# Sliding-window attention and a highway layer: key chunks shifted by half a block, scores packed by 64x64 quadrants

## The chip, the cores and the metric

The kernel runs on one core of one Trainium2 chip. The metric is the device time of one execution in microseconds. A profiled execution also gives a trace of each engine: TensorE (PE, with its weight loads as PEld), VectorE (DVE), ScalarE (ACT), GpSimd (POOL, which here mostly issues loads) and SyncE (SP, which issues stores).

## The reference

Two layers follow each other: attention in which each query sees the first four keys ("sinks") and the 128 latest, then a highway layer on the rows of all heads joined.

```python
# q, k, v: (B=4, H=8, S=768, D=64); n_sink = 4, window = 128
scores = (1 / sqrt(D)) * (q @ k.transpose(0, 1, 3, 2))
keep = (pos_k < n_sink) | ((pos_q - pos_k >= 0) & (pos_q - pos_k < window))
a = softmax(where(keep, scores, -1e9))
x = (a @ v).transpose(0, 2, 1, 3).reshape(B * S, H * D)      # 3072 x 512
h = maximum(x @ w_h, 0)
t = 1 / (1 + exp(-(x @ w_t + b_t)))
out = t * h + (1 - t) * x
```

## The kernel before

The 3072 rows are cut into 24 chunks of 128 (six per batch entry); chunk n is `n % 6` within its batch entry. A chunk goes through these steps, which the code names by engine:

- `load_qk`, `load_v` (lines 81, 90): POOL issues three DMAs that bring 128 rows of q, k and v for all heads and turn f32 into f16. `AHEAD = 8` chunks are loaded ahead.
- `pe_T` (193): eight transposes make q and k columns of 128 rows, two heads to a 128x128 block, in one PSUM tile from the pool `m_ps`; `act_T` (202) copies all 1024 columns to SBUF on ACT as `qk`.
- `pe_S` (233): scores, keys on partitions and queries on columns. The keys a query block can see lie in the chunk before and in its own chunk, so there are 256 score columns for each head, half of which the window masks. A chunk takes 16 matmuls, 8 for each half-chunk of four heads (half as many in the first chunk of a batch entry). Each head has 64 rows of contraction, so even heads use rows 0 to 63 of the array and odd heads rows 64 to 127, into different PSUM banks.
- `act_S` (248): exp of 1024 columns per half-chunk, twice a chunk. `dve_mask` (257): multiply by a 0/1 mask. The first chunk of a batch entry has only its own keys, 512 columns.
- `pe_sink`, `act_sink` (216, 226): scores of the four sinks of all heads for two chunks at once, needed for chunks 2 to 5 of a batch entry (`ks`, which `pool_sink` fills, line 207; sink values `vs` by `sink_v`).
- `pe_A` (267): 16 matmuls of 66 columns, e times v and a column that sums the weights; two more for the sinks. `dve_rec`, `dve_x` (292, 297): divide, giving `xh`.
- `pe_X`, `act_X` (309, 316): four transposes of `xh`, copied to SBUF by ACT as `xT`.
- `pe_Mh`, `pe_Mt` (337, 321): the two products with the weights, four matmuls of 512 columns each (and one for the bias). `act_u` (332): tanh. `dve_d`, `dve_e`, `dve_o` (345, 351, 357): the highway combination; SP stores 128 rows.

PSUM holds two score tiles of two banks (`ps_s`), one A tile of two banks (`ps_av`), and two banks (`ps_m`) that turn among transposes, sink scores, Mh and Mt. The order of the work on each engine is that of the program text: lines 379 to 486 write it out by hand, and each engine takes its instructions in that order. In the loop, iteration i does T(i+2), S(i+1), X(i-1), A(i), Mh(i-1), Mt(i-1) on PE; ACT takes qk(i+2), xT(i-1), the two exps of i+1, u(i-1); DVE takes the masks of i+1, ee, otok, rec, xh, dd. Iterations -2 to 1 are written apart for the start, where the first stage also multiplies zeros (`warm_up(8)`, `spare(3)`).

The POOL queue at the start (137 to 162) is: q0, k0, the identity's mask, v0, q1, k1, two selects that make the 0/1 mask, v1, the sink values, the weights w_t and w_h, two small selects, and then the further chunks. `more_constants` (166 to 178) is DVE work that waits for the mask.

Of the kernel before, what the change touches and what calls it, by code (L numbers as in the profile page):

```python
# [8 lines left out]
FP16 = mybir.dt.float16  # L9
# [7 lines left out]
_AVN = 66  # L17
# [3 lines left out]
def kernel(  # L21
# [40 lines left out]
    sd_pool = ctx.enter_context(tc.tile_pool(name="p_sd", bufs=AHEAD))  # L62
    qkT_pool = ctx.enter_context(tc.tile_pool(name="p_qkT", bufs=5))
    e_pool = ctx.enter_context(tc.tile_pool(name="p_e", bufs=5))
    r_pool = ctx.enter_context(tc.tile_pool(name="p_r", bufs=3))
    x_pool = ctx.enter_context(tc.tile_pool(name="p_x", bufs=7))
# [6 lines left out]
    NV = AHEAD + 4  # L73
    NS4 = H * NSINK
    KW = NHP * P + 32
    XBAR = ()
    LATE = 0
    v_ring = [const.tile([P, VW], FP16, tag=f"v{i}", name=f"v{i}") for i in range(NV)]
    qk_sd = {}

    def load_qk(n):
        b, c = divmod(n, NSC)
        rows = slice(c * P, (c + 1) * P)
        qsd = sd_pool.tile([P, H, D], FP16, tag="qsd", name="qsd")
        ksd = sd_pool.tile([P, H, D], FP16, tag="ksd", name="ksd")
        nc.gpsimd.dma_start(out=qsd, in_=q[b, :, rows, :].transpose([1, 0, 2]))  # L86
        nc.gpsimd.dma_start(out=ksd, in_=k[b, :, rows, :].transpose([1, 0, 2]))  # L87
        qk_sd[n] = (qsd, ksd)

    def load_v(n):  # L90
        b, c = divmod(n, NSC)
        rows = slice(c * P, (c + 1) * P)
        vt = v_ring[n % NV][:, 0:H * 65].rearrange("p (h e) -> p h e", e=65)
        nc.gpsimd.dma_start(out=vt[:, :, 0:D], in_=v[b, :, rows, :].transpose([1, 0, 2]))  # L94
# [8 lines left out]
    mask = const.tile([P, 2, P], FP16, tag="mask", name="mask")  # L103
    mask0 = const.tile([P, P], FP16, tag="mask0", name="mask0")
    mask1 = const.tile([P, 2, P], FP16, tag="mask1", name="mask1")
# [5 lines left out]
    ones_row = const.tile([P, P], FP16, tag="ones_row")  # L111
    ks_bd = [const.tile([P, KW], FP16, tag=f"ks{i}", name=f"ks{i}") for i in range(2)]
    vs_bd = [const.tile([P, H, 65], FP16, tag=f"vs{i}", name=f"vs{i}") for i in range(2)]
    vs_dn = [const.tile([NS4, D], FP16, tag=f"vd{i}", name=f"vd{i}") for i in range(2)]
    es_t = [const.tile([P, 2, P], FP16, tag=f"es{i}", name=f"es{i}") for i in range(2)]

    with tc.manual_schedule(engines={ENG.DVE}):
        nc.vector.memset(warm, 0.0)
        nc.vector.memset(ident, 1.0)
        nc.vector.memset(ebias, _EXP_BIAS)  # L120
        nc.vector.memset(mask, 1.0)
        nc.vector.memset(bm, 1.0)
        for vt in v_ring:
            init_v(vt)

    def load_sink_v(b):
        nc.gpsimd.dma_start(out=vs_dn[b % 2], in_=v[b, :, 0:NSINK, :])

    def sink_v(b, eng):
        eng.tensor_tensor(  # L130
            out=vs_bd[b % 2][0:NS4, :, 0:D], in0=vs_dn[b % 2].unsqueeze(1).to_broadcast([NS4, H, D]),
            in1=bm[0:NS4, :].unsqueeze(2).to_broadcast([NS4, H, D]), op=ALU.mult)
# [4 lines left out]
    with tc.manual_schedule(engines={ENG.Pool}):  # L137
        load_qk(0)
# [4 lines left out]
        load_qk(1)  # L143
        nc.gpsimd.affine_select(
            out=mask[:, 1, :], in_=mask[:, 1, :], compare_op=ALU.is_ge, fill=0.0,
            base=0, pattern=[[1, P]], channel_multiplier=-1)
        nc.gpsimd.affine_select(
            out=mask[:, 0, :], in_=mask[:, 0, :], compare_op=ALU.is_ge, fill=0.0,
            base=-1, pattern=[[-1, P]], channel_multiplier=1)
        load_v(1)  # L150
        load_sink_v(0)
        load_w(moe_w_t, wt_sb)
# [7 lines left out]
        load_qk(2)  # L160
        load_v(2)
        load_qk(3)

    nc.sync.dma_start(out=bt32, in_=moe_b_t.unsqueeze(0))

    def more_constants():
# [7 lines left out]
        nc.vector.tensor_copy(out=mask0, in_=mask[:, 1, :])  # L174
        nc.vector.memset(mask0[0:NSINK, :], 1.0)
        nc.vector.tensor_copy(out=mask1, in_=mask)
        nc.vector.memset(mask1[0:NSINK, 0, :], 1.0)
# [12 lines left out]
    qkT, tp_of, s_of, e_of, av_of, rec_of = {}, {}, {}, {}, {}, {}  # L190
    xtp_of, xh_of, xT_of, t_of, u_of, h_of, dd_of, ee_of, sk_of = {}, {}, {}, {}, {}, {}, {}, {}, {}

    def pe_T(n):
        qsd, ksd = qk_sd.pop(n)
        tp = m_ps.tile([P, 2 * NHP, P], FP16, tag="m", name="tp")
        for j in range(NHP):
            nc.tensor.transpose(tp[:, j, :], qsd[:, 2 * j:2 * j + 2, :], ident)  # L197
        for j in range(NHP):
            nc.tensor.transpose(tp[:, NHP + j, :], ksd[:, 2 * j:2 * j + 2, :], ident)  # L199
        tp_of[n] = tp  # L200

    def act_T(n):
        qk = qkT_pool.tile([P, 2 * NHP, P], FP16, tag="qk", name="qk")
        nc.scalar.copy(out=qk, in_=tp_of.pop(n))  # L204
        qkT[n] = (qk[:, 0:NHP, :], qk[:, NHP:2 * NHP, :])

    def pool_sink(b):
        _, kT = qkT[b * NSC]
        ks = ks_bd[b % 2]
        for hh in range(2):  # L210
            rows = slice(64 * hh, 64 * hh + 64)
            dst = ks[rows, 0:NHP * 136].rearrange("p (a b) -> p a b", b=136)
            nc.gpsimd.tensor_copy(out=dst[:, :, NSINK * hh:NSINK * hh + NSINK],
                                  in_=kT[rows, :, 0:NSINK])

    def pe_sink(n):
        ks = ks_bd[(n // NSC) % 2]
        sk = m_ps.tile([P, 2, P], FP32, tag="m", name="sk")
        for t in range(2):
            qT, _ = qkT[n + t]  # L220
            for hp in range(NHP):
                nc.tensor.matmul(sk[:, t, :], lhsT=ks[:, hp * P:(hp + 1) * P],
                                 rhs=qT[:, hp, :], start=(hp == 0), stop=(hp == NHP - 1))
        sk_of[n] = sk

    def act_sink(n):
        nc.scalar.activation(out=es_t[(n // 2) % 2][0:NS4], in_=sk_of.pop(n)[0:NS4], func=AF.Exp,
                             bias=ebias[0:NS4], scale=SCALE)

    def srcs_of(n):  # L230
        return ([] if n % NSC == 0 else [qkT[n - 1][1]]) + [qkT[n][1]]

    def pe_S(n, g):
        qT, _ = qkT[n]
        srcs = srcs_of(n)
        np_ = len(srcs)
        sps = s_ps.tile([P, 2, 512], FP32, tag="s", name="sps")
        for hl in range(2):
            hp = 2 * g + hl
            for pc, kk in enumerate(srcs):  # L240
                for hh in range(2):
                    rows = slice(64 * hh, 64 * hh + 64)
                    o = (hl * np_ + pc) * P
                    nc.tensor.matmul(sps[:, hh, o:o + P], lhsT=kk[rows, hp, :],  # L244
                                     rhs=qT[rows, hp, :], start=True, stop=True)
        s_of[n, g] = sps

    def act_S(n, g):
        np_ = 1 if n % NSC == 0 else 2
        sps = s_of.pop((n, g))  # L250
        e = e_pool.tile([P, 2, 2, np_, P], FP16, tag="e", name="e")
        nc.scalar.activation(out=e.rearrange("p a b c d -> p a (b c d)"),  # L252
                             in_=sps[:, :, 0:2 * np_ * P], func=AF.Exp,
# [3 lines left out]
    def dve_mask(n, g):  # L257
        c = n % NSC
        np_ = 1 if c == 0 else 2
        m = {0: mask0, 1: mask1.rearrange("p a b -> p (a b)")}.get(  # L260
            c, mask.rearrange("p a b -> p (a b)"))
        ev = e_of[n, g].rearrange("p a b c d -> p (a b) (c d)")
        nc.vector.tensor_tensor(  # L263
            out=ev, in0=ev, in1=m.unsqueeze(1).to_broadcast([P, 4, np_ * P]),
            op=ALU.mult)

    def pe_A(n, warm_n=0):
        b, c = divmod(n, NSC)
        vts = ([] if c == 0 else [v_ring[(n - 1) % NV]]) + [v_ring[n % NV]]
        av = av_ps.tile([P, 2, 4, P], FP32, tag="av", name="av")  # L270
        for _ in range(warm_n):
            nc.tensor.matmul(av[:, 0, :, :], lhsT=warm[:, 0:P], rhs=warm, start=True, stop=True)
        for g in range(2):
            e = e_of.pop((n, g))
            first = True
            for hl in range(2):
                for hh in range(2):
# [244 lines left out]
```

The softmax here doesn't subtract the row's maximum and nothing guards it: scores larger than these inputs give would overflow.

## Time and profile before

| | us |
|---|---|
| median of three runs | 130.05 (129.35 to 130.19) |
| the profiled execution, its own time | 129.52 |
| span of its trace, first to last instruction | 127.8 |
| first scores, S(0) | 7.97 |
| first A matmul of chunk 4 | 34.43 |
| first A matmul of chunk 23 | 115.78 |
| last output operation ends, on DVE | 124.4 |

The page of the profile gives each engine's busy time and its share of the span, the chain that ended last, and the costliest groups: line, engine, operation, tile written and read, count, then busy time, the mean duration of one in ns, and the idle time before them with what ended it. In the order of time, a row has the start and the length of a run of equal instructions. Matmuls overlap: a matmul's length is its passage through the array, and the next one starts long before it ends, so what a block costs is the distance to the start of the next block.

### The profile page before, as it was taken

To read this page: it belongs to the slowest core of one execution; us is meant where nothing else is said; L and a number is where in the kernel's file an instruction comes from. 1 tells how busy PE (TensorE), PEld (TensorE's weight loads), DVE (VectorE), ACT (ScalarE), POOL (GpSimd) and SP (SyncE) were. 2 spreads that over 40 slices of the span, in tenths; PEclk is the share of its full clock that TensorE was granted. 3 is DMA by queue.
4 is the path that set the end of the run, shared out by engine and by line. 5 is a ranking of instruction groups with operands and counts; after the bars stand their busy time and mean duration, and the time that the engine had idled before them with its cause. 6 is when DMAs were issued, how large, how long until landed. Compare 5 with 4: busy or idle time off the path is not lost.

```text
span 127.8 us, 3253 instructions
## 1 busy us (share of the span) xinstructions
PE 110.1 (86%) x1315; PEld 67.9 (53%) x1315; DVE 101.8 (80%) x214; ACT 97.6 (76%) x129; POOL 74.9 (59%) x98
## 2 busy tenths in 40 slices
PE   6758989569999899999998999999989999999620
PEld 2236434447755574586555656755655666564300
DVE  6544626495999898998998998989989999899760
ACT  4066435999897998998987989989969989893310
POOL 6999939999899989999999995005000000000000
PEclk9999999999999999999999999999999999999996
DMA  0999999999999999999999999922022202210222
GB/s 1 105 126 140 165 153 157 180 181 197 160 156 204 204 180 201 163 199 200 164 199 194 208 159 205 186 95 82 8 82 82 82 5 82 82 60 28 82 82 82
DMA packets 79728, 17.00 MB, mean 133 GB/s; under 512 B 75617, under 2 KB 76641, under 8 KB 79714
## 3 DMA queue, kind: packets, MB, share of 16 engines
q0 software_dynamic: 76256, 10.51, 122.6%
q1 hardware_dynamic: 3458, 6.30, 13.3%
q8 instruction: 10, 0.16, 0.5%
q14 instruction: 4, 0.03, 0.1%
HBM read 21.01 MB, written 6.29 MB: 214 GB/s over the span
## 4 chain that ended last, share of the span: by engine, by line
PE 39%; ACT 29%; DMA 12%; POOL 9%; DVE 6%; issue 3%; POOLq 0%; ACTq 0%
PE tps L328 14%; PE hps L341 11%; ACT qk L204 10%; DMA wh_sb<-in_moe_w_h_dram 7%; ACT u L334 6%; ACT e L252 6%; ACT xT L318 5%; DMA ksd<-in_k_dram 5%; PE tps L326 4%; POOL qsd L86 3%; PE sps L244 3%; PE av L280 2%; POOL ksd L87 2%; POOL v L94 2%; PE xtp L313 2%
## 5 line engine op out<-in xcount | busy, mean ns | idle before, releaser
L252 ACT ACTIVATE e<-sps,ebias 128x1024 f16<-128x1024 f32 (+1 forms) x48 | 48.6, 1054 | 1.8 <-PE sps L244 1.8
L263 DVE TENSOR_TENSOR e<-e,mask 128x1024 f16<-128x1024 f16 (+1 forms) x48 | 29.1, 640 | 4.7 <-ACT e L252 4.6
L204 ACT COPY qk<-tp 128x1024 f16<-128x1024 f16 x24 | 24.2, 1009 | 6.4 <-PE tp L199 6.4
L341 PE MATMUL hps<-wh_sb,xT 128*128 128x512 f16 x96 | 24.8, 380 | 3.4 <-ACT xT L318 2.9
L334 ACT ACTIVATE u<-tps 128x512 f16<-128x512 f32 x24 | 14.3, 597 | 16.0 <-PE tps L328 16.0
L328 PE MATMUL tps<-wt_sb,xT 128*128 128x512 f16 x96 | 25.0, 384 | 0.1
L86 POOL DMA_DIRECT2D qsd<-in_q_dram x24 | 22.4, 932 | 3.4 <-DMA wh_sb<-in_moe_w_h_dram 2.0
L94 POOL DMA_DIRECT2D v<-in_v_dram x24 | 22.3, 929 | 0.5 <-DVE dd L347 0.3
L347 DVE SCALAR_TENSOR_TENSOR dd<-hps,xh 128x512 f16<-128x512 f32 x24 | 16.6, 691 | 7.4 <-PE hps L341 5.7
L87 POOL DMA_DIRECT2D ksd<-in_k_dram x24 | 22.1, 920 | 0.5 <-PE tps L328 0.3
L353 DVE SCALAR_TENSOR_TENSOR ee<-u,dd 128x512 f16<-128x512 f16 x24 | 16.5, 689 | 3.5 <-ACT u L334 3.2
L280 PE MATMUL av<-v,e 128*128 128x66 f16 x352 | 17.7, 197 | 0.6 <-DVE e L263 0.5
L328 PEld LDWEIGHTS <-xT 128*128 128x128 f16 x96 | 9.4, 98 | 15.0 <-issue 4.1
L299 DVE TENSOR_TENSOR xh<-av,rec 128x512 f16<-128x512 f32 x24 | 16.6, 692 | 0.8
L359 DVE SCALAR_TENSOR_TENSOR otok<-xh,ee 128x512 f32<-128x512 f16 x24 | 16.6, 692 | 0.8
L280 PEld LDWEIGHTS <-e 128*128 128x128 f16 x352 | 15.2, 100 | 2.2 <-DVE e L263 1.9
L244 PE MATMUL sps<-qk 64*128 64x128 f16 x352 | 14.6, 223 | 1.5 <-ACT qk L204 1.5
L318 ACT COPY xT<-xtp 128x512 f16<-128x512 f16 x24 | 14.4, 598 | 0.4 <-PE xtp L313 0.3
L341 PEld LDWEIGHTS <-xT 128*128 128x128 f16 x96 | 7.9, 97 | 12.0 <-ACT xT L318 5.7
L244 PEld LDWEIGHTS <-qk 64*128 64x128 f16 x352 | 10.4, 97 | 4.8 <-ACT qk L204 1.4
L199 PE MATMUL tp<-ident,ksd 128*128 128x128 f16 x96 | 9.8, 227 | 1.7 <-DMA ksd<-in_k_dram 1.6
L197 PEld LDWEIGHTS <-qsd 128*128 128x128 f16 x96 | 7.2, 100 | 6.8 <-DMA qsd<-in_q_dram 2.2
(51 smaller groups left out, 100.2 us busy)
## 6 DMA issues: line engine op xcount, KB each, us to landing
out_dram<-otok SPq DMA_DIRECT2D x24, 256.0 KB, 4.5
qsd<-in_q_dram POOLq DMA_DIRECT2D x24, 128.0 KB, 6.5
ksd<-in_k_dram POOLq DMA_DIRECT2D x24, 128.0 KB, 6.5
v<-in_v_dram POOLq DMA_DIRECT2D x24, 128.0 KB, 6.7
wt_sb<-in_moe_w_t_dram POOLq DMA_DIRECT2D x1, 512.0 KB, 7.3
wh_sb<-in_moe_w_h_dram POOLq DMA_DIRECT2D x1, 512.0 KB, 9.4
vd<-in_v_dram POOLq DMA_DIRECT2D x4, 4.0 KB, 4.9
bt<-in_moe_b_t_dram SPq DMA_DIRECT2D x1, 2.0 KB
```

The source lines that it names most:

```text
L86: nc.gpsimd.dma_start(out=qsd, in_=q[b, :, rows, :].transpose([1, 0, 2]))
L87: nc.gpsimd.dma_start(out=ksd, in_=k[b, :, rows, :].transpose([1, 0, 2]))
L94: nc.gpsimd.dma_start(out=vt[:, :, 0:D], in_=v[b, :, rows, :].transpose([1, 0, 2]))
L204: nc.scalar.copy(out=qk, in_=tp_of.pop(n))
L244: nc.tensor.matmul(sps[:, hh, o:o + P], lhsT=kk[rows, hp, :], rhs=qT[rows, hp, :], start=True, stop=True)
L252: nc.scalar.activation(out=e.rearrange("p a b c d -> p a (b c d)"), in_=sps[:, :, 0:2 * np_ * P], func=AF.Exp, bias=ebias, scale=SCALE)
L263: nc.vector.tensor_tensor(out=ev, in0=ev, in1=m.unsqueeze(1).to_broadcast([P, 4, np_ * P]), op=ALU.mult)
L280: nc.tensor.matmul(av[:, g, 2 * hl + hh, 0:_AVN], lhsT=e[:, hh, hl, pc, :], rhs=vt[:, 65 * h:65 * h + _AVN], start=first, stop=False, skip ...
L318: nc.scalar.copy(out=xT, in_=xtp_of.pop(n))
L328: nc.tensor.matmul(tps, lhsT=xT[:, kc, :], rhs=wt_sb[:, kc, :], start=False, stop=(kc == NOC - 1))
L334: nc.scalar.activation(out=u, in_=t_of.pop(n), func=AF.Tanh)
L341: nc.tensor.matmul(hps, lhsT=xT[:, kc, :], rhs=wh_sb[:, kc, :], start=(kc == 0), stop=(kc == NOC - 1))
```

## The change

Keys and values are cut at other places than queries. Query chunk c still covers rows 128c to 128c + 127, but key chunk c covers rows 128c - 64 to 128c + 63 (`chunk_parts`). At the seam of two batch entries a key chunk has 64 rows of each, loaded by two DMAs; there are 25 key chunks instead of 24. The 128 queries of a block then see all of their own key chunk in part ("A"), the upper half of the queries sees the lower half of the next key chunk, and the lower half of the queries the upper half of the chunk before ("B"). The two B parts are 64x64 squares and share 64 columns, one on partitions 0 to 63 and one on 64 to 127, so a head has 192 score columns (`EW`) instead of 256.

The parts that change with it:

- exp, mask and `e` have 768 columns per half-chunk, in all chunks (the first chunk of a batch entry too, with its own mask).
- `pe_SA` takes 8 matmuls of 128 columns a chunk, `pe_SB` 16 of 64 columns on 64 rows and 64 columns of the array. `pe_AA` takes 8 and `pe_AB` 16 matmuls of 66 columns, the latter on 64x64 quadrants in pairs.
- `pe_T` transposes q or k in 64-row halves, 8 transposes of 64 columns for each, into the last 512 bytes of the two banks of a score tile, where 768 of 1024 columns are used. `act_T` copies 512 columns; q on ACT, k on ACT in the loop and mostly on DVE at the start.
- In the loop, T of chunk n+2 is hosted by the score tiles of chunk n; `xT` is copied by DVE; X(i) stands at the end of iteration i, and dd, ee, otok run for i-2.
- Sink scores are needed for chunk 1 too: two chunks at once in later batch entries, one at a time in the first. The four sink-value loads go to SP at the start.
- The start is written anew (`lone_T`, `lone_S`), w_h is loaded ahead of w_t, the three spare matmuls go, the pool sizes change (q/k landing 10, transposed q and k 7 each, x 5).

```diff
+    def chunk_parts(n):
+        b, c = divmod(n, NSC)
+        if c:
+            return [(slice(0, P), b, c * P - HP)]
+        return ([(slice(0, HP), b - 1, S - HP)] if b else []) + ([(slice(HP, P), b, 0)] if b < B else [])
...
-        load_qk(0)
+        nc.sync.dma_start(out=bt32, in_=moe_b_t.unsqueeze(0))
+        for b in range(B):
+            nc.sync.dma_start(out=vs_dn[b], in_=v[b, :, 0:NSINK, :])
+        load_q(0)
+        load_k(0)
+        load_k(1)
         nc.gpsimd.affine_select(
             out=ident, in_=ident, compare_op=ALU.is_equal, fill=0.0,
             base=0, pattern=[[-1, P]], channel_multiplier=1)
         load_v(0)
...
+        load_v(1)
+        load_q(1)
+        load_k(2)
+        tri(mask, slice(0, HP), 0, P, HP - 1, -1, 1)
+        tri(mask, slice(HP, P), 0, P, 0, 1, -1)
+        tri(mask, slice(0, HP), P, EW, 0, 1, -1)
+        tri(mask, slice(HP, P), P, EW, -1, -1, 1)
         load_w(moe_w_h, wh_sb)
...
+    def t_view(sps):
+        return sps.bitcast(FP16)[:, :, 4 * EW:4 * EW + 4 * HP].rearrange(
+            "p h (a b) -> p h a b", b=HP)
+
+    def pe_T(n, g, sd):
...
+        tv = t_view(s_tile(n, g))
+        for hp in range(NHP):
+            for hf in range(2):
+                rows = slice(HP * hf, HP * hf + HP)
+                nc.tensor.transpose(tv[:, hf, hp, :], sd[rows, 2 * hp:2 * hp + 2, :],
+                                    ident[rows, rows])
...
+    def pe_SA(n, g):
+        sps = s_tile(n, g)
         for hl in range(2):
             hp = 2 * g + hl
-            for pc, kk in enumerate(srcs):
+            for hh in range(2):
+                rows = slice(64 * hh, 64 * hh + 64)
+                nc.tensor.matmul(sps[:, hh, hl * EW:hl * EW + P], lhsT=kT[n][rows, hp, :],
+                                 rhs=qT[n][rows, hp, :], start=True, stop=True)
+
+    def pe_SB(n, g):
+        sps = s_tile(n, g)
+        prev = kT[n - 1] if n % NSC else kT[n]
+        for hl in range(2):
+            hp = 2 * g + hl
+            o = hl * EW + P
+            for part, kk, ks, qs in ((slice(0, HP), kT[n + 1], slice(0, HP), slice(HP, P)),
+                                     (slice(HP, P), prev, slice(HP, P), slice(0, HP))):
                 for hh in range(2):
                     rows = slice(64 * hh, 64 * hh + 64)
-                    o = (hl * np_ + pc) * P
-                    nc.tensor.matmul(sps[:, hh, o:o + P], lhsT=kk[rows, hp, :],
-                                     rhs=qT[rows, hp, :], start=True, stop=True)
+                    nc.tensor.matmul(sps[part, hh, o:o + HP], lhsT=kk[rows, hp, ks],
+                                     rhs=qT[n][rows, hp, qs], start=True, stop=True)
...
+    def pe_AB(n):
...
+        for j in range(H):
+            for src, part, vt, h in ((lo, hi, nxt, j), (hi, lo, prv, (j + 4) % H)):
+                nc.tensor.matmul(
+                    av[part, h // 4, h % 4, 0:_AVN], lhsT=e_at(n, h)[src, P:EW],
+                    rhs=vt[src, 65 * h:65 * h + _AVN], start=(h % 4 == 0), stop=False,
+                    skip_group_check=True)
...
+        for i in range(3, NB + 2):
+            n = i + 1
...
+            if on(n):
+                for g in range(2):
+                    if hosts and on(n + 2):
+                        pe_T(n, g, (q_sd, k_sd)[g].pop(n + 2))
...
+                    pe_SA(n, g)
+                for g in range(2):
+                    pe_SB(n, g)
+                act_S(n, 0)
+                if hosts and on(n + 2):
+                    act_T(n, 0, qT, n + 2)
+            if on(i):
+                dve_mask(i, 1) if i > 3 else None
+                if i > 3:
+                    act_X(i - 1, nc.vector.tensor_copy)
...
+            if 0 <= i - 2 and i > 3:
+                dve_d(i - 2)
+                dve_e(i - 2)
+            if on(i):
+                pe_AB(i)
+                pe_AA(i)
+                dve_rec(i)
+                dve_x(i)
+            if has_sink(n):
+                pe_sink(n)
+                act_sink(n)
+            if i > 3:
+                dve_o(i - 2)
+            if on(n):
+                dve_mask(n, 0)
+                act_S(n, 1)
+            if on(i - 1):
+                pe_Mt(i - 1)
+                act_u(i - 1)
+                pe_Mh(i - 1)
+            if on(n) and hosts and n + 2 <= NB:
+                act_T(n, 1, kT, n + 2)
+            if on(i):
+                pe_X(i)
```

The new start, ahead of this loop, runs in this order: T(q0), T(k0), T(k1), S(0), the masks of chunk 0, T(q1), T(k2), `sink_ones`, `sink_v`, `fill_ks` on DVE, A(0), S(1), the sinks of 1, X(0), A(1), Mh(0), X(1), Mh(1), T(q2), T(k3), S(2), Mt(0), the masks of 2, ee and otok of 0, Mt(1), ee and otok of 1, A(2), T(q3), T(k4), X(2), S(3), T(q4), T(k5).

## The prediction

> **What bounds the kernel now.** I read the page's engine shares first. Four engines work about three quarters of the span or more, so no share decides; the chain that ended last has to.
>
> ```profile
> PE 110.1 (86%) x1315; PEld 67.9 (53%) x1315; DVE 101.8 (80%) x214; ACT 97.6 (76%) x129; POOL 74.9 (59%) x98
> PE 39%; ACT 29%; DMA 12%; POOL 9%; DVE 6%; issue 3%; POOLq 0%; ACTq 0%
> ```
>
> The chain alternates between PE and ACT. TensorE in order of time shows how; the bracket is idle time before the row and what ended it.
>
> ```profile
> 91.77 1.04 PE L341 MATMUL hps<-wh_sb,xT 128*128 128x512 f16 x4 [0.26 <-ACT xT L318]
> 92.64 0.38 PE L326 MATMUL tps<-bt,ones_row 128*128 128x512 f16 x1
> 92.86 1.03 PE L328 MATMUL tps<-wt_sb,xT 128*128 128x512 f16 x4
> 93.72 0.39 PE L197 MATMUL tp<-ident,qsd 128*128 128x128 f16 x4
> 93.95 0.39 PE L199 MATMUL tp<-ident,ksd 128*128 128x128 f16 x4
> 94.27 0.62 PE L244 MATMUL sps<-qk 64*128 64x128 f16 x16
> 94.82 0.40 PE L313 MATMUL xtp<-ident,xh 128*128 128x128 f16 x4
> 95.05 0.42 PE L280 MATMUL av<-v,e 128*128 128x66 f16 x8
> 95.97 1.04 PE L341 MATMUL hps<-wh_sb,xT 128*128 128x512 f16 x4 [0.49 <-ACT xT L318]
> ```
>
> One chunk takes 95.97 - 91.77 = 4.20 us. PE waits 0.2 to 0.5 of it for xT, which ACT copies only after qk (0.9). That is the stall ahead of the loop. Between the first A of chunk 4 (34.43) and of chunk 23 (115.78) lie 19 chunks, 4.28 each (sink chunks are longer). Start-to-start distances give the true PE costs: four transposes 0.23 (56 ns each), 16 scores in 0.55, eight A matmuls about 0.26 (33 ns each), Mh 0.87, Mt with bias 1.08. In S, matmuls on rows 0-63 and 64-127 run as pairs: eight pairs of 56 ns are 0.45, and 0.10 is the change from 128-row to 64-row matmuls (four k transposes alone would have ended 0.09 before 94.27). I charge 0.095 for each change of shape.
>
> The rows that price the vector engines, and the start:
>
> ```profile
> L252 ACT ACTIVATE e<-sps,ebias 128x1024 f16<-128x1024 f32 x40 | 43.5, 1124 | 1.3 <-PE sps L244 1.3
> L263 DVE TENSOR_TENSOR e<-e,mask 128x1024 f16<-128x1024 f16 x40 | 26.0, 685 | 3.3 <-ACT e L252 3.3
> L299 DVE TENSOR_TENSOR xh<-av,rec 128x512 f16<-128x512 f32 x24 | 16.6, 692 | 0.8
> L318 ACT COPY xT<-xtp 128x512 f16<-128x512 f16 x24 | 14.4, 598 | 0.4 <-PE xtp L313 0.3
> L252 ACT ACTIVATE e<-sps,ebias 128x512 f16<-128x512 f32 x8 | 5.1, 704 | 0.5 <-PE sps L244 0.5
> L263 DVE TENSOR_TENSOR e<-e,mask 128x512 f16<-128x512 f16 x8 | 3.1, 419 | 1.4 <-ACT e L252 1.4
> ```
>
> ```profile
> 6.63 0.26 DVE L174 COPY mask<-mask 128x128 f16<-128x128 f16 x1 [1.71 <-POOL mask L144]
> 7.39 0.53 DVE L178 TENSOR_SCALAR bt<-bt 1x512 f16<-1x512 f32 x1
> 7.97 0.61 PE L244 MATMUL sps<-qk 64*128 64x128 f16 x8 [1.10 <-ACT qk L204]
> ```
>
> DVE sits in front of the mask until POOL has made it, then does small constants until 7.92; that queue matters below.
>
> **Steady state, engine by engine.** Independent instructions in a row overlap by 0.085 on DVE (dd 62.53 to mask 63.14, 0.61 for 0.692) and 0.105 on ACT (u 59.41 to qk 59.91).
>
> ACT: exp at 768 columns lies halfway between 704 and 1124, 0.914; two cost 1.62 net against 2.04. The qk copy (0.90) becomes two half copies of the xT kind (0.49 each); xT (0.49) goes; u 0.49 and es about 0.2 stay. 4.1 becomes 3.3. ACT stops being the limit, and its cover for PE's stall goes.
>
> DVE: the masks become 552 ns each by the same halving, 0.93 net for two. dd, ee, xh, otok 4 x 0.61, rec with its dependence 0.24, ee behind dd 0.12. That is 3.73, plus the xT copy, new on DVE. No row shows DVE copying f16 out of PSUM. Ends: 0.15 (an SBUF copy of 256 columns, line 176) and 0.69 (xh, 512 columns out of PSUM). I take 0.69, the nearer row, 0.61 net: 4.34 per chunk. At 0.15 it is 3.8.
>
> [...]
>
> PE per chunk without sinks, with the pairs priced by rows:
> - T: 16 transposes of 64 columns, 8 pairs. Bounds 33 ns (an A matmul of 66 columns) and 56 (an S pair) a pair; 33 taken: 0.27 (before 0.45).
> - SA: 8 matmuls, 4 pairs of 56: 0.22. SB: 16 quadrant matmuls as 8 pairs of 33: 0.26. Before, S was 0.45.
> - AB: 16 quadrant matmuls, 8 pairs of 33: 0.27; AA 8 x 33: 0.26; es matmuls 0.22. Before 0.53 + 0.22.
> - X 0.23, Mt 1.08, Mh 0.87 unchanged. Three shape changes (64-row, quadrant, full) 0.29, before two, 0.19.
>
> Sum 3.97; before 4.02. Sinks: five blocks of 0.224 a batch instead of four, and es matmuls for chunk 1 too. Per batch 6 x 3.97 + 1.12 - 0.22 = 24.7, so 4.1 a chunk. Nothing before shows a 64x64 quadrant. If all four run at once SB is 0.13 and AB 0.22 (-0.18 a chunk, 3.9). If quadrant pairs need 56, +0.37. If there is no pairing at all, T, SB and AB cost 16 x 33 each, +0.8.
>
> [...]
>
> So PE needs 4.1 and DVE 4.1 to 4.3 where the loop now takes 4.28. X(n) closes an iteration and now waits for xh of its own chunk and for u to free its bank; behind it stand the next T and S. By the order above xh ends 0.3 or more before Mh does, so this costs 0 to 0.2. The period I take is **4.28, no gain**.
>
> **Start, laid out in queue order with these durations.** POOL issues from 1.31: q0 1.07, half k0 0.75 (between 0.58 for vd and 0.9 for a whole block), k1 0.9, ident 0.3, half v0 0.75, v1, q1, k2 2.7, four mask selects 0.25 each: 8.9 instead of 6.6. DVE stands before the mask copies and their memsets (1.5): 10.4. Only behind these stands k0's copy, which S(0) needs: S(0) at 10.9 instead of 7.97, **+2.9**. The POOL queue, not landing, sets this: k1, the third issue, lands near 6.7.
>
> From there steps that overlapped stand in line. Before rec(0) DVE now has k2's copy, the ones, sink_v and two ks copies (1.8): xh(0) 16.4 (11.6 before), A(1) 17.6, xh(1) 19.7, Mh(0), X(1), Mh(1) until 21.7, T(2,3), S(2) 22.8, A(2) 26.2; four output operations precede rec(2): xh(2) 29.2, k4's copy, S(3) 29.7; T(4,5) wait for score banks until exp(3) at 32.1; S(4) 32.9, A(3) 33.6, Mt(2), Mh(2) until 36.6; X(3), T(5), T(6), S(5), A(4) **39.5**, against 34.43 (A(3) stood at 29.76). Loss 5.0. Bounds: 4.0 if the selects and memsets are 1 us shorter; 7 if PE stays at the slow spacing of the first stage (four transposes 0.61 at 6.26, 0.39 from 16.86), since the three spare matmuls are gone. The loads that this point needs (q7, k7) land near 34, so they do not hide it.
>
> The POOL issues that later batches gain by halves (8 more, four vd moved to SP) ride beside loads that run 20 us ahead: nothing. If that cover were gone, 0.75 each.
>
> **Sum.** 39.5 + 19 x 4.28 + tail. From A(23) at 115.78 to the end is 12.0 (last otok 124.4, then its store); after, the last two iterations have the same steps, 12.0. Span 132.8. The profiled execution took 129.52 for 127.8, so 134.5; the median of the runs is 0.5 above it, hence 134.8, +3.7%. Its own range, DVE copy 0.43 to 0.69 and pairs within a few ns: 131.5 to 138.
>
> **Rivals.**
> 1. Faster: the xT wait vanishes and quadrants really run four at once, with a cheap DVE copy. For: ACT drops to 3.3, DVE can reach 3.8, PE 3.9. Period 3.9: 19 x 0.38 = 7.2 gained, 4 to 5 lost at the start, 127 to 128. It decides once the period falls below 4.28 - 5.0/19 = **4.02**. Against: PE is then busy without a gap. 15%, with 12% more that start and period cancel within 1% of 130.05 (129 to 131.4).
> 2. PE becomes the bound through slow quadrant loads: 56 ns a pair, period 4.6: +0.33 x 24 = 8 on the start's 5, 139 to 143. 16%.
> 3. The packing does not do what it says: tiles do not run side by side, PE per chunk 4.9 with sinks, 147 or more. Against: S shows pairs 64 rows each at 56 ns. 7%.
> My forecast holds 50%.
>
> About 1% is what a measurement of this kernel tells from no change. Faster 0.15, same 0.12, slower 0.73. The range 128.0 to 143.0 leaves out the best of rival 1 and rival 3.
>
> **What would show it.** Right: S(0) near 11 and A(4) near 39 to 40; PE rows without idle for xT; ACT idle about 1 us a chunk; xT copies on DVE 0.43 to 0.69; SB starting in pairs 33 ns apart. Wrong: A(4) before 37 (the start overlaps better than my line), a period below 4.0, or PE matmul groups of SB and AB longer than 0.27 each.

## The result and the profile after

The changed kernel takes 135.28 us, median of four runs (134.23 to 137.11), against 129.7 for the kernel before on the same chip. Executions of one kernel fall into a faster and a slower group some 2% apart, and every ratio in this document compares the faster ones alone, while medians are over all. The ratio is 1.0355, 95% interval 1.0255 to 1.0455: slower, by about the 3.7% of the forecast. The profiled execution took 134.23 us (forecast 134.5) for a span of 132.5 (forecast 132.8).

The page of the changed kernel: shares of the engines, the granted clock in 40 slices, the chain that ended last.

```profile
PE 112.5 (85%) x1984; PEld 70.2 (53%) x1984; DVE 106.4 (80%) x249; ACT 81.7 (62%) x133; POOL 76.4 (58%) x102
...
PEclk9999999996579999999999999999999999999996
...
DVE 48%; PE 32%; ACT 7%; POOL 6%; issue 4%; DVEq 0%; POOLq 0%; ACTq 0%
```

Three things are new. ACT falls from 76% to 62% and leaves the chain (29% to 7%). DVE takes its place (6% to 48%). And TensorE's granted clock has a dent near 33 us that the kernel before has not: there the clock, once up at 16.4 us, stays up to the last matmuls. The row's digits ahead of the first recorded rise (20.9 us in the changed kernel) must not be read as full speed: eight half transposes take 0.21 there (5.33 to 5.54 us), and 0.12 at 23.02.

The groups of DVE and ACT by tile shape: count, busy us and mean ns, idle time before.

```profile
L298 DVE TENSOR_TENSOR e<-e,mask 128x768 f16<-128x768 f16 x48 | 25.8, 570 | 5.5 <-ACT e L290 5.5
L355 DVE COPY xT<-xtp 128x512 f16<-128x512 f16 x21 | 8.8, 418 | 0.1
```

```profile
L290 ACT ACTIVATE e<-sps,ebias 128x768 f16<-128x768 f32 x48 | 42.5, 896 | 21.3 <-PE sps L285 21.3
```

Exp and mask are near what halving predicted (914 and 552; a common mask takes 552, and the mean of 570 contains one slow one). The xT copy is not: 418 ns, where the forecast took 690. DVE in order of time, one chunk of the loop of the changed kernel (start, us, engine, line, operation):

```profile
65.59 1.02 DVE L298 TENSOR_TENSOR e<-e,mask 128x768 f16<-128x768 f16 x2
66.53 0.42 DVE L355 COPY xT<-xtp 128x512 f16<-128x512 f16 x1
66.87 0.68 DVE L382 SCALAR_TENSOR_TENSOR dd<-hps,xh 128x512 f16<-128x512 f32 x1
67.65 0.69 DVE L388 SCALAR_TENSOR_TENSOR ee<-u,dd 128x512 f16<-128x512 f16 x1
68.26 0.20 DVE L336 RECIPROCAL rec<-av 128x8 f32<-128x8 f32 x1
68.50 0.69 DVE L341 TENSOR_TENSOR xh<-av,rec 128x512 f16<-128x512 f32 x1
69.10 0.70 DVE L394 SCALAR_TENSOR_TENSOR otok<-xh,ee 128x512 f32<-128x512 f16 x1
```

No row carries a bracket, so DVE waits for nobody. The next pair of masks starts at 69.73, 4.14 us behind the first row: the sum of DVE's work is the period, which is 4.11 us in most chunks (from one reciprocal to the next). TensorE in the same view, later:

```profile
83.04 0.29 PE L229 MATMUL sps<-ident,qsd 64*128 64x64 f16 x8
83.17 0.28 PE L272 MATMUL sps<-t,t 64*128 64x128 f16 x4
83.28 0.28 PE L229 MATMUL sps<-ident,ksd 64*128 64x64 f16 x8
83.40 0.28 PE L272 MATMUL sps<-t,t 64*128 64x128 f16 x4
83.60 0.32 PE L285 MATMUL sps<-t,t 64*64 64x64 f16 x16
83.76 0.66 PE L312 MATMUL av<-v,e 64*64 64x66 f16 x16
```

From start to start, 8 half transposes take 0.12 to 0.13, 4 SA matmuls 0.11 (the second four 0.20 with the change to quadrants behind them), and the 16 quadrant matmuls of SB 0.16: four quadrants run at once. The last row contains a wait; the same group takes 0.36 to 0.39 in chunks without one.

For what follows I use three marks of each profiled execution: the start of chunk 4's reciprocal (end of the start phase), the time from it to chunk 23's, and where the granted clock is 0.5 behind its first rise. The tail behind chunk 23's reciprocal is 9.6 to 10.2 everywhere.

| kernel | median us | rec(4) | rec(4) to rec(23) | clock 0.5, us |
|---|---|---|---|---|
| before | 129.7 | 35.35 | 82.22 | none |
| changed | 135.28 | 42.89 | 79.97 | 31.1–37.9 |
| e1_warm_gap | 133.68 | 43.15 | 79.26 | 7.9–21.5, 35.2–38.6 |
| e2_k0_on_act | 135.37 | 45.38 | 79.40 | 9.5–30.0, 36.8–40.2 |
| e3_xT_on_act | 133.92 | 43.02 | 78.79 | 31.3–38.1 |
| e4_sb_twice | 138.59 | 46.15 | 81.34 | 9.9–30.4, 37.2–40.6 |
| e5_warm_start | 135.75 | 44.83 | 79.15 | 13.1–30.2 |
| e6_start_order | 134.16 | 42.71 | 80.51 | 8.5–32.4 |
| e7_start_xT_act | 133.91 | 43.05 | 78.25 | 9.2–33.1 |
| e8_before_no_spare | 130.06 | 35.92 | 82.22 | none |
| e9_fill_full | 134.74 | 44.37 | 79.27 | 9.7–30.1 |
| e10_fill_small | 136.37 | 43.53 | 78.70 | 31.4–38.2 |
| e11_start_filled | 133.40 | 36.13 | 85.62 | 48.6–55.4 |
| e12_start_filled_loads | 126.74 | 37.85 | 77.54 | 18.5–25.3 |

The change against before: start +7.5, loop -2.25, tail -0.6, span +4.7. One trace stands for each kernel. Six runs below (e1, e2, e5, e6, e9, e10) leave the loop as the changed kernel has it, and theirs took 78.7 to 80.5: the gain over 82.22 is there in each, but a difference of 1 us between two totals of the loop says little by itself.

### The profile page after: what moved, and what is told of

It reads as the page before. It is cut to its first block, busy times and chain, and to the rows that moved or that the text cites. A ratio compares the mean times of both kernels' runs of the same rounds, so it can differ in the third digit from the quotient of the medians.

```text
span 132.5 us, 4673 instructions
## 1 busy us (share of the span) xinstructions
PE 112.5 (85%) x1984; PEld 70.2 (53%) x1984; DVE 106.4 (80%) x249; ACT 81.7 (62%) x133; POOL 76.4 (58%) x102
## 4 chain that ended last, share of the span: by engine, by line
DVE 48%; PE 32%; ACT 7%; POOL 6%; issue 4%; DVEq 0%; POOLq 0%; ACTq 0%
DVE e L298 11%; DVE ee L388 9%; DVE otok L394 8%; DVE xh L341 8%; PE hps L376 7%; DVE dd L382 6%; PE tps L363 6%; ACT e L290 4%; DVE xT L355 4%; PE av L322 3%; PE av L312 3%; PE sps L229 2%; PE sps L272 2%; PE sps L285 2%; PE xtp L350 2%
## 5 line engine op out<-in xcount | busy, mean ns | idle before, releaser
L290 ACT ACTIVATE e<-sps,ebias 128x768 f16<-128x768 f32 x48 | 42.5, 896 | 21.3 <-PE sps L285 21.3
L298 DVE TENSOR_TENSOR e<-e,mask 128x768 f16<-128x768 f16 x48 | 25.8, 570 | 5.5 <-ACT e L290 5.5
L234 ACT COPY t<-sps 128x512 f16<-128x512 f16 x43 | 24.8, 577 | 8.0 <-PE sps L229 8.0
L382 DVE SCALAR_TENSOR_TENSOR dd<-hps,xh 128x512 f16<-128x512 f32 x24 | 16.4, 682 | 1.9 <-PE hps L376 1.9
L272 PE MATMUL sps<-t,t 64*128 64x128 f16 x192 | 13.1, 229 | 4.2 <-DVE t L234 3.3
L394 DVE SCALAR_TENSOR_TENSOR otok<-xh,ee 128x512 f32<-128x512 f16 x24 | 16.4, 684 | 0.1
L312 PE MATMUL av<-v,e 64*64 64x66 f16 x384 | 13.2, 199 | 2.3 <-DVE e L298 1.4
L312 PEld LDWEIGHTS <-e 64*64 64x64 f16 x384 | 9.8, 113 | 4.1 <-DVE e L298 2.6
L350 PEld LDWEIGHTS <-xh 128*128 128x128 f16 x96 | 7.3, 99 | 8.1 <-issue 2.7
L322 PE MATMUL av<-v,e 128*128 128x66 f16 x192 | 11.1, 201 | 0.2 <-issue 0.2
L350 PE MATMUL xtp<-ident,xh 128*128 128x128 f16 x96 | 9.5, 222 | 1.6 <-DVE xh L341 1.6
L361 PE MATMUL tps<-bt,ones_row 128*128 128x512 f16 x24 | 9.4, 390 | 0.5 <-DVE xT L355 0.5
```

The costliest lines, as they stand in the source:

```text
L234: (eng or nc.scalar.copy)(out=t.rearrange("p a (h b) -> p h a b", b=HP), in_=t_view(s_tile(n, g)))
L290: nc.scalar.activation(out=e.rearrange("p a b c -> p a (b c)"), in_=s_tile(n, g)[:, :, 0:2 * EW], func=AF.Exp, bias=ebias, scale=SCALE)
L298: nc.vector.tensor_tensor(out=ev, in0=ev, in1=m.unsqueeze(1).to_broadcast([P, 4, EW]), op=ALU.mult)
L312: nc.tensor.matmul(av[part, h // 4, h % 4, 0:_AVN], lhsT=e_at(n, h)[src, P:EW], rhs=vt[src, 65 * h:65 * h + _AVN], start=(h % 4 == 0), sto ...
L382: nc.vector.scalar_tensor_tensor(out=dd, in0=h_of.pop(n), scalar=0.0, in1=xh_of[n], op0=ALU.max, op1=ALU.subtract)
L394: nc.vector.scalar_tensor_tensor(out=otok, in0=xh_of.pop(n), scalar=2.0, in1=ee_of.pop(n), op0=ALU.mult, op1=ALU.add)
```

## The experiments

### What bounds the loop: e3 and e4

e3 gives the loop's xT copy back to ACT, ahead of the first exp.

```diff
+                act_X(i - 1)
                 act_S(n, 0)
...
-                    act_X(i - 1, nc.vector.tensor_copy)
```

> The changed kernel with the xT copy of the loop back on ACT, ahead of the first exp of the iteration, where ACT idles 0.8 us. Theory A (DVE's queue, 4.11 us a chunk, sets the loop): DVE's share falls by 0.33 a chunk, PE with about 3.9 becomes the bound, period 3.9 to 4.0 in chunks without sinks instead of 4.11, the time 2 to 3 us shorter. Rival B (PE sets the loop and DVE only keeps pace): period stays 4.1, the time within 0.7 us. Rival C (the copy on ACT delays the exps and brings the old stall back): period 4.2 or more, slower.

133.92 us, ratio to before 1.0324 (1.0262 to 1.0387). This interval overlaps that of the changed kernel, so the totals do not tell the two apart, and the 2 to 3 us of theory A did not come. The periods tell more. Both profiled executions have nearly the same clock and start (43.02); the median distance from one reciprocal to the next falls from 4.11 to 3.90, with 3.77 in several chunks. Two long ones, 5.28 and 5.64, take most of that back, and the loop is only 1.2 shorter. In both TensorE stands idle among the products with v, 0.79 and 1.18 us, for nothing that the profile shows; the changed kernel stands at the same two places for 0.63 and 0.23. The cause was not settled.

e4 computes all SB matmuls of the loop twice (the same values into the same places).

```diff
-                for g in range(2):
+                for g in (0, 0, 1, 1):
                     pe_SB(n, g)
```

> The changed kernel with every 64x64 score matmul of the loop issued twice (same result, 16 more quadrant matmuls a chunk, 336 in all). It prices the quadrants and asks what bounds the loop. The trace has 16 of them in 0.155 us, so the added work is 0.12 to 0.15 a chunk. Theory A (DVE bounds the loop, PE has about 0.2 of slack): period stays 4.11, the time rises by less than 0.7 us. Rival B (PE bounds the loop): period rises by 0.12 to 0.15, the time by 2.5 to 3.2 us. If quadrants do not run four at once as the trace says, 0.26 to 0.5 a chunk.

138.59 us, ratio to before 1.0702 (1.065 to 1.0754). The 16 additional quadrant matmuls cost TensorE 0.13 a chunk (32 in 0.28 instead of 16 in 0.15), and most periods stay at 4.11. The profiled execution, 138.82 us, is 4.6 above the changed kernel's: 1.4 lie in the loop, in a few longer chunks, and 3.3 in the start, where the clock was at 0.5 until 30.4. The clock need not be all of that: another execution of e4, with a mean granted clock of 0.968, took 137.51, against the changed kernel's 134.23 at 0.965. Neither theory held whole. Together with e3: DVE sets the pace in the common chunk, and TensorE has little slack behind it. Quadrant loads are no bound.

### The start: e1, e2, e5

e2 copies k0's transposes on ACT, so that S(0) does not stand behind DVE's mask constants.

```diff
-        act_T("k0", 1, kT, 0, nc.vector.tensor_copy)
+        act_T("k0", 1, kT, 0)
```

> The changed kernel with the first copy of k0 on ACT instead of DVE, where it stands behind the mask constants. Theory A (that queue is what delays S(0)): S(0) starts at 8.0 to 8.2 instead of 10.75; the masks are still ready only at 10.3, so rec(0) moves from 15.56 to about 13.5 and the time falls by 1 to 2 us. Rival B (the later chain, not chunk 0, sets the start): S(0) moves the same, rec of chunk 3 and the end move by less than 0.5.

Chunk 0's reciprocal comes at 13.05 instead of 15.56, near what was priced, and nothing of it arrives in the total: 135.37 us. TensorE in order of time, products of chunk 1:

```profile
17.18 0.65 PE L312 MATMUL av<-v,e 64*64 64x66 f16 x16 [2.49 <-DMA v<-in_v_dram]
```

The 2.5 us gained are waited for v2, whose load POOL issues behind the 512 KB of w_h; in the changed kernel the same products run from 17.16, with a wait for a mask until 17.95. The clock of this execution was at 0.5 from 9.5 to 30.0. The four executions of e2 include one of 134.10 at a mean granted clock of 0.965, where the changed kernel has 134.23 at 0.965. So the +2.9 of the forecast's first step is real, and next to nothing is gained by removing it alone.

e1 puts seven matmuls on zeros into TensorE's wait ahead of X(2), e5 24 of them into four waits.

```diff
         lone_T(3, 4)
+        warm_up(7)
         pe_X(2)
```

> The changed kernel with seven matmuls of zeros put into TensorE's 1.8 us wait before X(2). Theory A (the wait lets the granted clock fall to one half from about 31 to 38 us, which is the part of the start's loss that the prediction had not): the clock row shows 1.0 in that stretch, S(3) to A(4) run at the fast spacing, rec of chunk 4 comes near 40.5 instead of 42.9, and the time falls by 2 to 2.5 us, to about 132. Rival B (the start waits for ACT and DVE there, the slow clock is covered): the clock is 1.0 and the time falls by less than 0.7. Rival C (the clock falls whatever this wait is): nothing changes.

> Edit: the changed kernel with 24 matmuls on zeros in the start's waits of TensorE: 8 behind k1's transposes, 7 ahead of chunk 2's xh transposes, 5 ahead of and 4 behind the transposes of q4 and k5. They compute nothing that is used. Theory A (the size of the start's loss that the forecast missed is the granted clock, and the clock falls where TensorE stands idle): the record shows 1.0 from about 21 us on with no stretch at 0.5 behind it (the changed kernel: 0.5 from 31.1 to 37.9 us), chunk 4's reciprocal starts 1.5 to 2.5 us earlier than 42.9 (40.4 to 41.4), and the time is 132 to 133.7, against 135.3 for the changed kernel. Theory B (the start is a chain of waits on ScalarE, VectorE and loads, and TensorE's speed in it decides little): the clock may well stay at 1.0, chunk 4's reciprocal stays within 0.7 us of 42.9, and the time is 134.5 to 135.5. Theory C (the fillers lie on the chain, since TensorE takes its work in order): chunk 4's reciprocal later than 43.5 and 136 or more.

e1: 133.68 us, but chunk 4 is not earlier (43.15); the slow stretch moved from 31.1 to 35.2. e5: 135.75 us, against 132 to 133.7 in theory A; the clock rose at 6.3, fell at 13.1 and rose only at 30.2; behind that it held through the stretch where the changed kernel loses it. Its four times lie between 131.81 and 136.42. So fillers decide something, but not as "TensorE must not stand idle": the next runs settle what.

### What sets the granted clock: e9, e10, e8

In the trace of the changed kernel the granted clock is on record for 10.24 us at 1.0 (from 20.86), 6.83 at 0.5 and 92.16 at 1.0, in that of the kernel before for 109.23 at 1.0 (from 16.45): 3, 2, 27 and 32 times 3.41 us. For stretches of 3.41 us that end where these records do, I added up the columns of all matmuls, each times the share of the 128x128 array that it uses. As full use I count 512 columns per 0.216 us, the distance of the five matmuls of Mt and its bias (1.08), which makes 8090 in 3.41 us. The stretch from 27.7 us in the changed kernel: AA 8x66, es 2x260, T 16x64 by 1/2, X 4x128, SA 4x128 by 1/2, SB 8x64 by 1/4: 2456, use 0.30. The clock fell behind it.

e9 puts 3 full matmuls on zeros ahead of X(2) and 3 ahead of the transposes of q4 and k5; e10 the same number with 32 rows and 32 columns of weights, which keeps TensorE as long (three in a row take 0.82 us in both) and uses 1/16 of the array.

```diff
         lone_T(3, 4)
+        warm_up(3)
         pe_X(2)
...
         dve_mask(3, 1)
+        warm_up(3)
         lone_T(4, 5)
```

> Edit: the changed kernel with 3 matmuls of 128x128 weights by 512 columns on zeros ahead of chunk 2's xh transposes and 3 more ahead of the transposes of q4 and k5, both in waits of TensorE. They compute nothing that is used. Read from the runs so far: if every matmul counts with its columns times the share of the 128x128 array that it uses, the windows of 3.41 us after which the granted clock fell had 0.30 of full use or less, those after which it stayed had 0.32 or more, and the clock rose after windows of 0.40 and more. Theory A (this use sets the clock): the window from about 27.7 us goes from 0.29 to 0.48 and the next from about 0.3 to 0.5, so the record shows 1.0 from about 21 us to the end; chunk 4's reciprocal at 41 to 42.3 instead of 42.9, and a time of 133.3 to 134.8, against 135.3 for the changed kernel; the clock was then worth 0.6 to 2 us of the start's loss. Theory B (the clock falls for other reasons, the length of a wait among them: the two waits are shortened by less than half each): a stretch at 0.5 remains between 28 and 40 us.

> Edit: as the run before, but the 3 and 3 matmuls on zeros use 32 rows and 32 columns of the array by the same 512 columns of data, so that TensorE is busy for the same time and 1/16 of the array is used. Theory A (the use of the array sets the clock): use rises by 0.01 only, to about 0.30, and the clock falls to 0.5 from about 31 to 38 us as in the changed kernel; chunk 4's reciprocal at 42.7 to 43.5, time 135 to 136. Theory B (TensorE's busy time sets the clock, whatever part of the array is used): no stretch at 0.5 behind 21 us, the same times as the run with full matmuls.

Windows view, stretches between those points (us, busy us and instructions of PE, PEld, DVE, ACT, POOL, then granted clock, DMA share, GB/s). The changed kernel:

```profile
27.70:31.10 3.40, 1.82 (x44) 1.15 (x42) 2.88 (x6) 1.18 (x4) 2.71 (x4) 1.00 2.77 158
31.10:34.50 3.40, 2.72 (x64) 1.76 (x58) 1.45 (x3) 2.57 (x5) 3.40 (x5) 0.50 1.98 203
```

e10, small matmuls:

```profile
28.00:31.40 3.40, 2.57 (x49) 1.32 (x45) 2.73 (x6) 1.18 (x3) 3.39 (x5) 1.00 2.33 180
31.40:34.80 3.40, 2.94 (x37) 1.34 (x35) 1.54 (x3) 2.55 (x5) 3.40 (x5) 0.50 2.04 200
```

e9, full matmuls:

```profile
30.10:33.60 3.50, 2.94 (x52) 1.58 (x51) 3.01 (x7) 1.42 (x3) 3.38 (x5) 0.99 1.68 147
33.60:37.00 3.40, 2.74 (x54) 1.59 (x56) 1.58 (x4) 2.87 (x5) 3.40 (x5) 1.00 1.84 185
```

In e10 TensorE is busy for 2.57 of 3.40 us (1.82 without the fillers) and the clock falls all the same: the use is 0.31. In e9 it is busy for 2.94 and 2.74 and the clock holds: 0.54 and 0.48. e9's profiled execution had risen early and fallen again (9.7 to 30.1), against the expectation, so its total says little; its shortest of four runs took 131.74, e10's 133.57, the changed kernel's 134.23. Chunk 2 to chunk 4 took 11.8 with the clock held (e9), 12.3 in e5, and 13.3 to 14.0 where it fell (changed kernel, e1, e2, e3, e4, e10).

Two other runs are a closer pair with e9. In e2 the clock rose at 30.0, as in e9 at 30.1, and there are no fillers:

```profile
33.40:36.80 3.40, 2.17 (x54) 1.43 (x52) 1.45 (x3) 2.87 (x5) 3.40 (x5) 1.00 1.81 180
```

The use in this stretch is 0.28, and the clock fell behind it, at 36.8; e4 did the same (rise at 30.4, fall at 37.2, use 0.29).

By the same count the clock rose in the kernel before at 16.4 us behind a use of 0.43, and in the changed kernel at 20.9 and 37.9 behind 0.39 and 0.47. It stayed at half at 34.5 behind 0.27, and while it was up it held behind 0.43 and more in both, up to the last matmuls. How a matmul at the edge of a stretch is shared out moves a sum by some 0.02. TensorE's busy time orders the cases otherwise: the clock fell in e10 behind 2.57 of 3.40 us busy, held in the kernel before with 2.44 of 4.00 (24 to 28 us), and stayed at half in e12 behind 3.12 of 3.40 (18.5 to 21.9). That the use is the cause, and not something that goes with it, rests on e9 against e10 and e2; whether rows, columns or both count is not shown, since e10's matmuls have fewer of both.

e8 takes the three spare matmuls out of the kernel before.

```diff
-                spare(3)
```

> Edit: the kernel before the change without the three matmuls on zeros that it has between chunk 0's xh transposes and chunk 1's products with v. They compute nothing that is used. Theory A (the clock of the kernel before is held up by them: TensorE's idle stretches in the start are near the point where the clock falls): the record shows full clock later than the 16.6 us of the kernel before, or a stretch at 0.5 behind it, and the time is 131 to 133. Theory B (its TensorE is dense enough in the start without them): record and time as before, 129.3 to 130.3.

130.06 us, ratio 1.0027 (1.0004 to 1.005). The first rise comes later (20.2 instead of 16.4), with no fall behind it: the lowest use there is 0.43 before and 0.5 in e8. The kernel before does not live on its spares.

### A start that is written for its loads: e6, e7, e11, e12

e6 rewrites the order of chunks 0 to 4 (the same instructions), issues q, k, v of the first chunks ahead of the weights, and copies k0 on ACT; e7 is e6 with e3's edit. The loads of e6:

```diff
-        load_w(moe_w_h, wh_sb)
...
-        load_v(2)
+        load_v(3)
         load_q(2)
         load_k(3)
-        load_w(moe_w_t, wt_sb)
-        load_v(3)
+        load_k(4)
+        load_v(2)
+        load_q(3)
+        load_w(moe_w_h, wh_sb)
+        load_q(4)
+        load_k(5)
+        load_w(moe_w_t, wt_sb)
+        load_v(4)
```

> Edit: the changed kernel's loop from chunk 4 on as it is; the instructions of chunks 0 to 4 ahead of it are the same but in another order (scores and transposes of the next chunk ahead of the matmuls with the weights, k0's copy on ScalarE, the mask constants' selects behind k2's load), and the loads of chunks 1 to 4 are issued ahead of the two weight loads. Theory A (the start's loss of 7.5 us is order: work that waits in line behind other work): chunk 4's reciprocal at 36 to 39 us instead of 42.9, the steady part as before (80 us from chunk 4's to chunk 23's reciprocal), and a time of 129 to 132. Theory B (the start is bounded by its loads: about 1 MB of weights and 2 MB of q, k and v at the 150 GB/s of the first 30 us end no earlier whatever the order): chunk 4's reciprocal at 41 or later, waits of TensorE on the loads of weights or of q and k in the place of the present ones, and 133.5 to 136.

> Edit: the reordered start of the run before, and the loop's copy of xT on ScalarE ahead of the first exp instead of on VectorE. Theory A (the two gains lie in different stretches, the start and VectorE's sum in the loop, and add up): 1.0 to 1.6 us less than the run with the reordered start alone, so 128 to 130.5 if that one gives 129 to 132; at 128.5 or less it would be below the kernel before the change (129.7). Theory B (once VectorE is relieved TensorE or ScalarE's order bounds the loop, or the early loop is short of loads): no gain, within 0.5 us of the run with the reordered start alone.

e6: 134.16 us, chunk 4 at 42.71, no gain. TensorE in order of time:

```profile
15.11 0.39 PE L243 MATMUL sps<-ident,qsd 64*128 64x64 f16 x8 [2.61 <-DMA qsd<-in_q_dram]
17.33 0.39 PE L243 MATMUL sps<-ident,ksd 64*128 64x64 f16 x8 [1.83 <-DMA ksd<-in_k_dram]
```

It waits for q2 and k3 with the products of chunk 0 in line behind them, and the clock was at 0.5 from 8.5 to 32.4. e7's loop is 2.3 shorter than e6's (78.25 against 80.51), its median only 0.25; with runs from 133.06 to 135.93 the total is inconclusive.

e11 is e7 with the products of chunks 0 and 1 ahead of those transposes, v2, k4, q2, k3 ahead of the weights, and 18 full matmuls on zeros in the waits of the first 18 us.

```diff
+        warm_up(8)
         pe_T(("q", 2), 0, q_sd.pop(2))
```

> Edit: another order of chunks 0 to 4 ahead of the loop (products with v of chunks 0 and 1 ahead of the transposes of q2 and k3; loads of v2, q2, k3, q3, k4 ahead of the weights), with 18 matmuls on zeros in TensorE's waits of the first 18 us, and the loop's xT copy on ScalarE. Theory A (the run with the reordered start lost its gain to the clock, which was at 0.5 from 8.5 to 32.4 us): no stretch at 0.5 between 20 us and the end, chunk 4's reciprocal at 36 to 39 us instead of 42.7, and a time of 127.5 to 130.5, level with the kernel before the change or below it. Theory B (loads or VectorE bound the start): chunk 4's reciprocal at 41 or later in spite of the clock, and 132.5 to 134.

The start does what was asked: full clock from 7.6 us, chunk 4 at 36.13, 6.8 us earlier. The time moves little (133.40, where theory A had 127.5 to 130.5), because the loop gives most of it back in one place. TensorE in order of time:

```profile
49.57 1.04 PE L272 MATMUL sk<-t,ks 128*128 128x128 f16 x8 [4.32 <-POOL ks L261]
```

The copy of the sink keys of the second batch entry stands in POOL's line behind the issues of the loads up to chunk 12. From 28.9 to 49.05 us POOL issues them one behind the other, some 0.9 us each, and is idle for only 1.7. In the changed kernel POOL gets there no sooner (48.05), but the sink scores that need the copy start at 50.48 there, so nobody waits. e12 puts the loads of chunks 5 to 7 in the order of their use and issues the loop's loads 5 chunks ahead:

```diff
-            load_set(i + AHEAD)
+            load_set(i + 5)
```

> Edit: the run before with the loads of chunks 5 to 7 in the order of their use, and with the loop's loads issued 5 chunks ahead instead of 8, so that GpSimd's copy of the sink keys for the second part of the batch does not stand in line behind loads that wait for free buffers (in the run before, TensorE waited 4.32 us for it at 49.6 us and chunk 7's reciprocal came 11.45 us after chunk 6's instead of 3.8). Theory A (that line is all that took the start's gain back): chunk 4's reciprocal at 36 us as there, no period over 5.5 us in the loop, 78 to 79.5 us from chunk 4's to chunk 23's reciprocal, and a time of 126 to 128, below the kernel before the change (129.7) by 1.3 to 2.8 percent. Theory B (the loads bound the early loop: about 384 KB a chunk at the 155 GB/s of the first 50 us): waits of TensorE for loads of q, k or v between 36 and 60 us, and 129.5 or more.

126.74 us, six runs from 125.93 to 127.56, ratio to before 0.9756 (0.9712 to 0.9801): below both kernels, as theory A had it. The copy of the sink keys now comes at 37.99. Its page:

```profile
PE 112.3 (90%) x2002; PEld 68.5 (55%) x2002; DVE 99.3 (79%) x227; ACT 94.0 (75%) x155; POOL 75.3 (60%) x102
...
PE 66%; DVE 16%; POOL 8%; DMA 4%; issue 2%; ACT 1%; DVEq 0%; POOLq 0%
```

With the start at 37.85 and the xT copy on ACT, TensorE is the bound (66% of the chain), and the loop takes 77.54, against 82.22 before. e12 changes several things at once; what each is worth in it was not measured, and such an order of loads was not tried on the kernel before.

## Why the prediction was right, and by which errors

The total was right by two errors of opposite sign, 2.3 us each; that they cancel is luck. In the forecast's own terms, first products of chunk 4 and 23 in the traces:

| term | forecast | measured |
|---|---|---|
| A(4) | 39.5 | 41.83 |
| 19 periods | 19 x 4.28 = 81.3 | 19 x 4.16 = 79.0 |
| tail from A(23) | 12.0 | 11.7 |
| span | 132.8 | 132.5 |

1. **The start**, "Loss 5.0", was mis-sized: 7.4. The first step was exact: S(0) at 10.75 (10.9), behind the mask selects and constants. The rest slipped: A(2) at 27.28 (26.2), A(4) at 41.83. The clock was at 0.5 from 31.1 to 37.9, and holding it is worth 1.2 to 1.7 us between chunk 2 and 4 by the numbers above. The bound of 7 had a slow TensorE in it, but for the first stage and for missing spares; e8 shows that the kernel before does not need them. What differs is the use: the new transposes and scores take a half or a quarter of the array, and with a wait of 1.6 us in it a stretch of 3.41 us comes to 0.30, while the lowest stretch of the kernel before, once its clock is up, has 0.43. The remaining 0.7 to 1.2 fit the 1.1 us by which A(2) was late already; what they are made of was not settled.

2. **The period**, "4.28, no gain", was mis-sized: 4.16 over all chunks, 4.11 in a common one. The term that was off is "I take 0.69, the nearer row" for DVE's copy of f16 out of PSUM; it took 0.418. No run shows the 0.43 for this copy at the lower end of the forecast's own range, nor the 4.1 for DVE that goes with it; in their place the changed kernel showed 0.418, and 4.11 for a chunk in which DVE has no gap. That DVE, no longer ACT, sets the pace was in the sum; the gapless rows of DVE and the shorter periods of e3 show it.

3. **The quadrants**, "If all four run at once SB is 0.13 and AB 0.22": SB 0.16, AB about 0.26 (0.36 less 0.1 for the change of shape). The slow quadrant loads of rival 2 are not seen: at its 56 ns a pair, 16 quadrant matmuls would take 0.45; they took 0.16. Nor do they start in pairs 33 ns apart, as the sign of being right had it, but four at a time. Rivals 2 and 3 fall with it.

4. **Rival 1**, faster once the period is below 4.02, was the nearest miss. Its condition did not come, since DVE stops at 4.11. It does not come in e12 either, whose 19 periods average 4.05 (A(4) at 36.79, A(23) at 113.74); e12 is faster because its start loses 2.4 instead of 7.4, which moves the break-even up to 4.28 - 2.4/19 = 4.15.

5. The cost set at nothing held: no wait of the loop of the changed kernel ends with a late load, though e11 shows how near POOL's queue is to the path.

6. Two slips of addition did not matter: the issues ahead of the masks sum to 8.8 instead of 8.9, and 134.5 with 0.5 on top is 135.0 instead of 134.8.

## What to carry to other kernels

Price an edit's start and its loop apart: here a loop that gained 2 us sat behind a start that lost 7, and the start was an order of instructions and loads that could be rewritten. A copy moved to another engine needs its own row; the nearest row of another operation was 0.69 here, and the copy took 0.418. And smaller matmul tiles did not only take less time here: the start they left had a thin stretch (use 0.30) behind which the clock fell to half, where the kernel before kept full speed from its first rise on.

## What the runs showed that was not expected

- **The clock went with the use of the array, not with TensorE's busy time**: it fell behind a use of 0.30 in the changed kernel and of 0.31 in e10, where TensorE was busy for 2.57 of 3.40 us, and held behind 0.54 and 0.48 in e9.
- **The same program has several clock histories in its start.** The first rise came at 20.9, 21.0 and 21.2 us in some profiled executions (changed kernel, e3, e10), but at 4.5 to 6.5 in e1, e4 and e9, whose instructions are the same up to there, followed by half speed from 8 or 10 us to between 21 and 30. Each execution's mean granted clock is on record, and within one kernel it differs like the times: the changed kernel has 134.23 us at 0.965, 134.23 at 0.920, 136.33 at 0.983 and 137.11 at 0.902, e9 131.74 at 0.937 and 135.91 at 0.996. A mean does not say when the clock was low, and it counts the time ahead of the first rise as full, so which history costs how much is argued, not shown.
- **DVE and POOL held each other up while POOL multiplied.** A mask at 70.2 us took 1389 ns instead of 552, while POOL built the sink values. The rows of both engines in the changed kernel:

```profile
69.73 1.86 DVE L298 TENSOR_TENSOR e<-e,mask 128x768 f16<-128x768 f16 x2
```

```profile
69.95 1.23 POOL L145 TENSOR_TENSOR vs<-vd,bm 32x512 f16<-32x512 f32 x1
```

Two masks otherwise take 1.02. e1 and e4 show one such mask each (1391 and 1390 ns). Elsewhere it hits ee or otok, which like the mask read nothing from PSUM: in e12 one otok took 1497 ns and two ee 1251 and 1266, instead of 681 and 693. In the changed kernel one ee took 931, beside POOL's instruction at 92.60. It went the other way too: in e9 POOL's instruction took 1509 ns instead of 1032, and the four DVE operations beside it kept their times. In the changed kernel dd, which reads PSUM, kept its time beside POOL's instructions at 49.20 and 92.60: 675 and 683 ns, with a mean of 682.
- **Matmuls of different quadrants started 3 to 4 ns apart** in SB of the changed kernel (at 83.60 us), four at a time; a change of tile shape cost TensorE about 0.1 us there (0.20 for four SA matmuls ahead of the quadrants, 0.11 without a change behind them).
